# Longer runs of the two feed-forward products in two row groups, a fourth chunk of attention turned by DMA, and one copy of neighbour rows left whole

## The chip, the cores and the metric

The kernel runs on one core of one Trainium2 chip. The metric is device time in microseconds, the median of several executions of the whole program. One further execution was recorded by the hardware profiler; all rows shown below come from that one, and its times count from the start of its span.

## The reference

```python
x = A_x                                            # [1, 2048, 640], float32
xn = layernorm(x)
q, k, v = split(xn @ wqkv)                         # 32 heads of 20
logits = sum_d q[s] * k[s - 2*w] * 20**-0.5        # w = 0..7: a window of 8 rows, every second row
logits = where(s - 2*w >= 0, logits, -1e9)
o = sum_w softmax(logits)[w] * v[s - 2*w]
s = o @ wo                                         # [2048, 640]
h = silu(xn @ w1)                                  # [2048, 1536]
g = silu(h @ w2)                                   # [2048, 640]
return x + s * g
```

Weights are `wqkv` [640, 1920], `wo` [640, 640], `w1` [640, 1536], `w2` [1536, 640].

## The kernel before

**Rows.** The 2048 rows are worked in four groups of 512, `g` = 0 to 3 (two halves of the sequence, times the even and the odd rows, since the window takes every second row). A group lies on 128 partitions with `T` = 4 rows of one parity on each. A row's window reaches seven rows of its parity back, so the last rows of partition p are needed on partitions p+1 and p+2.

**Precision.** Every operand of a product is split into a high and a low float32r part; a product is three matmuls (high·high, low·high, high·low). `TH`/`TL` hold the turned (transposed) input of a group, `OH`/`OL` the turned attention output, `SH`/`SL` the hidden values in a ring of `NS` = 3, `WR` the weights, high and low beside each other, in a ring of `RING` = 7 tiles `w_75` to `w_81`.

**A group.** First the Q/K/V product in four quarters `q` of eight heads each (`qkv_phase`): 20 units of three matmuls, in PSUM banks `acc`; ScalarE then copies a quarter's keys and values to `KV[q]` (L733) and its queries to `Q[q]` (L736, L739). `halo` then copies the last rows of each partition's keys and values to the next two partitions, on SyncE's queue (L751): 4 rows by one partition, 3 rows by two. Each of these two copies is cut in two at row 112 of its rows, so a quarter has four transfers of 112, 15, 112 and 14 partitions. Attention itself (`scores`, `values`) is VectorE's work, in the background, and runs on into the next group. Then the feed-forward (`ffn_phase`): `up` units (L1130 to L1132: w1, into a bank `rot`, of which there are two; ScalarE takes silu twice, L1143 and L1144, VectorE the low part, L1145) and `down` units (L1003, L1005: w2, accumulated over all 12 units in six `acc` banks). Behind the first `up` stands the wo product of the group before (`wo_phase`), and its result is multiplied into the gate tile `G`; GpSimd adds the residual (L1049) from `xr` tiles that SyncE's queue loads (L1048).

**Turning.** A chunk of 128 columns of x or of the attention output `O` is turned in one of two ways. On TensorE (`split_t`, L636): four transposes into a `rot` bank. By DMA (`send`, `join`): ScalarE sorts the chunk into 16-bit halves in one buffer (L668), two DMA transposes on SyncE's queue write a second buffer (L672), ScalarE sorts them back into the first (L681) and rounds the high part (L685), VectorE takes the low part (L686). `ON_DMA` says, by group and quarter, which chunks of the group before are sent and joined when.

**Weights.** In the first rounds weights come raw, are split, and the split form is stored to DRAM (`half_...`, L581 on SyncE's queue); later they are loaded split, by GpSimd's queue (L564), into the tile of the ring that comes free. A load waits until TensorE has used the tile's old content and, where that was a first-round unit, until its store has landed. The five wo units of `g` = 2 are such units (tiles `w_77` to `w_81`).

**Order.** TensorE's order is written out: `units`, from `plan(g)`. All other engines' orders come from a planner in the kernel (`Weave`), which simulates the five engines and eight DMA lanes with its own costs and due times, and adds constraints where TensorE would wait. The engines run their orders as built, each strictly in order.

Of the kernel before, what the change touches and what calls it, by code (L numbers as in the profile page):

```python
# [15 lines left out]
P = 128  # L16
S, D, F, H, DH = 2048, 640, 1536, 32, 20
W = 8
DC, FC = D // P, F // P
NQ = 4  # L20
HQ = H // NQ
CQ = HQ * DH
# [7 lines left out]
CA, CB = 384, 256  # L30
RING = 7
NS = 3
SINGLE = 6
RAW_AHEAD = 10
TURNS = 1
FIRST_AT = 44.0, 60.0
# [6 lines left out]
SUB_LATE = 3  # L43
ADD_LATE = 3
X_BY = {1: 2, 3: 0, 4: 1}
PACE0, PACE = -20.0, 12.0
WARM, WARM2 = 20, 3
HOLD = 3.4
# [11 lines left out]
BY_ACT = (0,)  # L60
IN_PARTS = 2
KEYS_FIRST = ((3, 0),)
QAT = 48
MORE = 32
OAT = 16
# [233 lines left out]
def local_attention_silu_ffn(ctx: ExitStack, tc: tile.TileContext, x, wqkv, wo, w1, w2, out):  # L299
# [9 lines left out]
    xg = x.rearrange("b (g p j) d -> (b g) p j d", p=P, j=J)  # L309
    og = out.rearrange("b (g p j) d -> (b g) p j d", p=P, j=J)  # L310
    OL_AT = {10: 2}
    groups = [(h, par) for h in range(2) for par in range(2)]
    NG = len(groups)

# [38 lines left out]
    SF = sb.tile([P, TOK], F32, name="sf")  # L353
    TURN = sb.tile([P, TOK], F32, name="turn")
# [6 lines left out]
    XP = [("xp", k, h) for k in range(DC) for h in range(2)]  # L361
# [27 lines left out]
    def free_for(old, new):  # L389

        add("DVE", 0.0, lambda: None, [], list(old) + list(new), 0)
# [8 lines left out]
    clock = [0.0]  # L400
# [13 lines left out]
    def plan(g):  # L414

        last = g == NG - 1
        todo = [("w1", 0)] + [("wo", 0)] * (g > 0)
        down = 0  # L420
        f = 1
        while f < FC:
            k = f // 2
            pair = f + 1 < FC and not (last and f > SINGLE)
            if g < TURNS and 1 <= k <= DC and k - 1 not in X_DMA:
                todo.append(("x", k - 1))
            if last and f in OL_AT:
                todo.append(("o", OL_AT[f]))
            if last and f == FC - 1:
                todo.append(("rest", (0, 1)))  # L430
            n = 2 if pair else 1
            todo += [("w1", u) for u in range(f, f + n)]
            f += n
            todo += [("w2", u) for u in range(down, down + n)]
            down += n
        return todo + [("w2", u) for u in range(down, FC)]

# [15 lines left out]
    def store_at(u):  # L455

        return 1 + (u[0] == "wo" or u[0] == "q" and u[2] % 2)
# [15 lines left out]
    for u in units:  # L473
        n = seen[u] = seen.get(u, 0) + 1
        at = store_at(u)
# [8 lines left out]
    def start(i):  # L484

        return QAT if i < first_q else 0

# [203 lines left out]
    def turn_x(c, i, at):  # L691
        keys = [("xin", t) for t in range(T)]
        by = (TURN, ("turn",)) if c not in X_BY else (piece(G, X_BY[c]), ("buf", X_BY[c]))
        to = piece(G, c), ("buf", c)
# [3 lines left out]
    def spare(s, q):  # L698

        return KV[q][:, s, HALO:, :].rearrange("p t m -> p (t m)")[:, :TOK], (("own", "val")[s], q, "x")  # L700

    def lend(s, q, back=False):
        k = ("own", "val")[s]
        lent = [[(k, q, t) for t in range(T)], both((k, q, "x"))]
        free_for(*(lent[::-1] if back else lent))
# [6 lines left out]
    def turn_o(g, c, i, out, into, at=0.0):  # L712

        qs = range(c * P // CQ, ((c + 1) * P - 1) // CQ + 1)
        keys = [("o", q, t) for q in qs for t in (0, 2)]
        xp = [(piece(XIN, k), ("xp", k)) for k in range(DC)]
        by, to = ((xp[0], xp[1]), (xp[2], xp[3]), (xp[4], (TURN, ("turn",))), (xp[1], xp[3]), (xp[0], xp[2]))[c]
        if g < NG - 1:
            by, to = ((TURN, ("turn",)), (SF, ("sf",))) if c % 2 == 0 else (xp[3], xp[4])
        if out:  # L720
            send(O, c, keys, "o", by, to, at)
        if into:
            join(to, by[0].rearrange("p (t n) -> p t n", t=T), both(by[1]), [], i, c, OH[i][:, c, :], OL[i][:, c, :], at)


    def q_keys(q, t):
        return [("q", q, t)] + [("q", q, t, k) for k in range(q if q == NQ - 1 else 0)]
# [14 lines left out]
    def halo(g, q):  # L742
        h, par = groups[g]
        kv = KV[q]
        own = kv[:, :, HALO:, :]
        kown = [(k, q, t) for k in ("kv", "own", "val") for t in range(T)]

        def shift(by, dst, src, tag, s=slice(0, 2), also=()):
            cut = 112
            for a, b in ((0, cut), (cut, P - by)):  # L750
                dma(lambda a=a, b=b: nc.sync.dma_start(kv[a + by:b + by, s, dst], own[a:b, s, src]),  # L751
                    kown, [("halo", q, tag, a, *also)], (b - a) * (s.stop - s.start) * CQ * 4 * (dst.stop - dst.start), clock[0],
                    quick=(g, q) in KEYS_FIRST)
        for part in ((slice(0, 1),), (slice(1, 2), ["v"])) if (g, q) in KEYS_FIRST else ((),):
            shift(1, slice(HALO - T, HALO), slice(0, T), 1, *part)
            shift(2, slice(0, HALO - T), slice(2 * T - HALO, T), 2, *part)
        c = carry[par]
        if h == 0:
            dma(lambda: nc.sync.dma_start(c[:, q], own[P - 2:P]), kown, [("carry", par, q)], 10240, clock[0] + 20)
        else:  # L760
            dma(lambda: nc.sync.dma_start(kv[0:1, :, HALO - T:HALO, :], c[1:2, q]), [("carry", par, q)],
                [("halo", q, 3, 0)], 5120, clock[0])
            dma(lambda: nc.sync.dma_start(kv[0:2, :, 0:HALO - T, :], c[:, q, :, 2 * T - HALO:, :]),
                [("carry", par, q)], [("halo", q, 4, 0)], 7680, clock[0])
# [163 lines left out]
    def qkv_phase(g, i, io):  # L928
        if g == TURNS:
            for c in O_FIRST:  # L930
                by, to = (((TURN, ("turn",)), spare(1, 0)), (spare(0, 1), spare(1, 1)))[c]
                join(to, by[0].rearrange("p (t n) -> p t n", t=T), both(by[1]), [], io, c, OH[io][:, c, :], OL[io][:, c, :])
            for v in ((0, 0), (0, 1), (1, 0), (1, 1)):
                lend(*v, True)
        if g == NG - 1:
            free_for([("xin", t) for t in range(T)], XP)
        if g in ON_DMA and g < NG - 1:
            free_for(["sf"], [("sf", 0), ("sf", 1)])
            free_for([("xin", 2), ("xin", 3)], XP[6:])
        for q in range(NQ):  # L940
            if g == 0 and q == 0:
                ps = first_quarter(i)
            else:
                turn_now(g, q, io)
                ps = [bank() for t in range(T)]
                for c in range(DC):
                    wh, wl, kh, kl = w_next("q", q, c)
                    for t in range(T):
                        o, kp = ps[t]

                        n = wh.shape[-1]

                        def unit(c=c, t=t, o=o, wh=wh, wl=wl, n=n):
                            o = o[:, :n]
                            hi, lo = TH[i][:, c, tsl(t)], TL[i][:, c, tsl(t)]
                            nc.tensor.matmul(o, hi, wh, start=c == 0, stop=False)  # L956
                            nc.tensor.matmul(o, lo, wh, start=False, stop=False)  # L957
                            nc.tensor.matmul(o, hi, wl, start=False, stop=c == DC - 1)  # L958
                        pe(3 * mm(n), unit, t_keys(i, [c], [t]) + [kh, kl], [kp])
                    w_done()  # L960
                    if g:
                        for k in (ON_DMA[g][1] if g in ON_DMA else O_AT).get((q, c), ()):
                            o_chunk(g - 1, k, io)
            if g == 0:
                add("POOL", 2.0, lambda q=q: nc.gpsimd.memset(KV[q][0:2, :, 0:HALO, :], 0.0), ["first"] if q else [],
                    [("halo", q, 1, 0), ("halo", q, 2, 0), ("halo", q, 3, 0), ("halo", q, 4, 0)], 1 + 12 * q)
            for t in range(T):
                evac_qkv(g, q, t, *ps[t])
            halo(g, q)
            scores(g, q)  # L970
            if q:
                values(g, q - 1)
        values(g, NQ - 1)
        turn_now(g, NQ, io)
        if g in ON_DMA and g < NG - 1:
            free_for([("sf", 0), ("sf", 1)], ["sf"])
            free_for(XP[6:], [("xin", 2), ("xin", 3)])

    def turn_now(g, q, io):
        for step in ON_DMA[g][0].get(q, ()) if g in ON_DMA else ():  # L980
            k, into, at = step
            turn_o(g, k, io, not into, into, clock[0] + at)

    def t_keys(i, cs, ts=range(T), kinds=("th", "tl")):
        return [(k, i, c, t) for k in kinds for c in cs for t in ts]

    ON_DMA = {1: ({0: ((0, 0, 4.0),), 1: ((0, 1, 8.0),)}, {(2, 4): (2, 3), (3, 4): (4,)}),
              NG - 2: ({0: ((0, 0, 4.0), (1, 0, 4.0)), 1: ((0, 1, 8.0), (1, 1, 8.0), (2, 0, 4.0)), 2: ((2, 1, 8.0),)},
                       {(2, 4): (3,), (3, 4): (4,)}),
              NG - 1: ({0: ((0, 0, 4.0), (1, 0, 4.0)), 1: ((0, 1, 8.0), (1, 1, 8.0)), 2: ((2, 0, 4.0), (3, 0, 4.0)),  # L990
                        3: ((2, 1, 8.0), (3, 1, 8.0))}, {(3, 4): (4,)})}
    O_AT = {(1, 4): (0,), (2, 4): (2, 3), (3, 4): (4,)}
# [267 lines left out]
```

## Time and profile before

| | |
|---|---|
| median of 3 runs | 624.95 us (624.53 to 624.99) |
| the profiled execution's own time | 624.74 us |
| its span, first to last instruction | 623.0 us |
| mean granted TensorE clock | 1.000 |
| busy: TensorE, VectorE, ScalarE, GpSimd | 617.8, 541.4, 267.7, 114.9 us |
| share of the chain that ended last: TensorE | 98% |
| moved by DMA | 166.86 MB, 268 GB/s |

The profiled execution's time is 1.74 us above its span: what lies before the first and after the last instruction. A row of the chain of work that ended last gives start, length and what ran; a row of the timeline gives start, length, engine, line, operation, tiles, and in brackets the idle time of that engine before it and what ended it. A row of the waits gives the sum, the number and the longest of the waits.

### The profile page before, as it was taken

To read this page: it belongs to the slowest core of one execution; us is meant where nothing else is said; L and a number is where in the kernel's file an instruction comes from. 1 tells how busy PE (TensorE), PEld (TensorE's weight loads), DVE (VectorE), ACT (ScalarE), POOL (GpSimd) and SP (SyncE) were. 2 spreads that over 40 slices of the span, in tenths; PEclk is the share of its full clock that TensorE was granted. 3 is DMA by queue.
4 is the path that set the end of the run, shared out by engine and by line. 5 is a ranking of instruction groups with operands and counts; after the bars stand their busy time and mean duration, and the time that the engine had idled before them with its cause. 6 is when DMAs were issued, how large, how long until landed. Compare 5 with 4: busy or idle time off the path is not lost.

```text
span 623.0 us, 9035 instructions
## 1 busy us (share of the span) xinstructions
PE 617.8 (99%) x3403; PEld 558.4 (90%) x3403; DVE 541.4 (87%) x545; ACT 267.7 (43%) x493; POOL 114.9 (18%) x165
## 2 busy tenths in 40 slices
PE   9999999999999999999999999999999999999997
PEld 7888999998889989999888999999988999999997
DVE  7599899999788999899949999989937999898834
ACT  5445555364545224563543604174644353252220
POOL 4800000001110142111221115112222211111100
PEclk9999999999999999999999999999999999999999
DMA  9999999599999989975999999999699999688652
GB/s 296 310 309 318 331 387 375 195 325 267 297 285 317 322 241 319 234 231 139 227 270 258 351 341 304 162 245 355 171 235 270 286 332 269 197 235 246 184 190 86
DMA packets 102873, 166.86 MB, mean 268 GB/s; under 512 B 34365, under 2 KB 64541, under 8 KB 102829
## 3 DMA queue, kind: packets, MB, share of 16 engines
q1 hardware_dynamic: 76333, 86.56, 52.1%
q0 software_dynamic: 25952, 79.31, 45.3%
q8 instruction: 27, 0.44, 0.3%
q10 hardware_dynamic: 544, 0.41, 0.2%
q14 instruction: 17, 0.14, 0.1%
HBM read 107.91 MB, written 34.16 MB: 228 GB/s over the span
## 4 chain that ended last, share of the span: by engine, by line
PE 98%; DMA 0%; DVE 0%; issue 0%
PE acc L1003 22%; PE acc L1005 15%; PE acc L956 10%; PE acc L958 10%; PE acc L957 10%; PE rot L1131 9%; PE rot L1132 9%; PE rot L1130 9%; PE acc L893 2%; PE rot L636 1%; DMA xin<-in_A_x_dram 0%; PE rot L877 0%; PE rot L1116 0%; DVE st L862 0%; PE rot L836 0%; DVE gate L1084 0%
## 5 line engine op out<-in xcount | busy, mean ns | idle before, releaser
L1003 PE MATMUL acc<-w,sh 128*128 128x384 f32 x384 | 113.2, 334 | 0.0
L956 PE MATMUL acc<-w,th 128*128 128x512 f32 (+2 forms) x300 | 113.0, 377 | 0.0
L958 PE MATMUL acc<-w,th 128*128 128x512 f32 (+2 forms) x300 | 112.9, 376 | 0.0
L957 PE MATMUL acc<-w,tl 128*128 128x512 f32 (+2 forms) x300 | 112.8, 376 | 0.0
L776 DVE TENSOR_TENSOR pr<-q,kv 128x2560 f32<-128x2560 f32 x32 | 90.3, 2821 | 22.8 <-DMA kv<-kv 22.6
L1005 PE MATMUL acc<-w,sh 128*128 128x256 f32 x384 | 107.1, 279 | 0.0
L1143 ACT ACTIVATE sh<-rot 128x512 fp32r<-128x512 f32 x48 | 28.8, 599 | 155.4 <-PE rot L1132 155.3
L1130 PE MATMUL rot<-th,w 128*128 128x512 f32 x240 | 94.4, 393 | 0.0
L1132 PE MATMUL rot<-th,w 128*128 128x512 f32 x240 | 93.9, 391 | 0.0
L1131 PE MATMUL rot<-tl,w 128*128 128x512 f32 x240 | 93.8, 391 | 0.0
L810 DVE TENSOR_TENSOR pr<-q,kv 128x2560 f32<-128x2560 f32 x32 | 91.9, 2871 | 0.8
L779 DVE TENSOR_REDUCE l<-pr 128x128 f32<-128x2560 f32 x32 | 89.9, 2810 | 0.2
L564 POOL DMA_DIRECT2D w<-half_q x52 | 37.4, 719 | 234.5 <-DVE pr L815 97.1
L564 POOL DMA_DIRECT2D w<-half_w x72 | 38.9, 541 | 201.7 <-PE acc L1005 86.4
L815 DVE TENSOR_TENSOR pr<-pr 128x1280 f32<-128x1280 f32 x64 | 74.0, 1155 | 1.2
L1005 PEld LDWEIGHTS acc<-w,sh 128*128 128x128 f32 x384 | 72.2, 188 | 1.0
L1003 PEld LDWEIGHTS acc<-w,sh 128*128 128x128 f32 x384 | 72.1, 188 | 1.0
L958 PEld LDWEIGHTS acc<-w,th 128*128 128x128 f32 x300 | 56.3, 188 | 8.8
L956 PEld LDWEIGHTS acc<-w,th 128*128 128x128 f32 x300 | 56.3, 188 | 8.7
L957 PEld LDWEIGHTS acc<-w,tl 128*128 128x128 f32 x300 | 56.3, 188 | 8.7
L733 ACT ACTIVATE kv<-acc 128x320 f32<-128x320 f32 x64 | 28.0, 440 | 75.9 <-PE acc L958 74.5
L1003 PE MATMUL acc<-w,sl 128*128 128x384 f32 x192 | 57.8, 332 | 0.0
(115 smaller groups left out, 1040.3 us busy)
## 6 DMA issues: line engine op xcount, KB each, us to landing
w<-half_w POOLq DMA_DIRECT2D x72, 640.0 KB, 7.3
w<-half_q POOLq DMA_DIRECT2D x39, 512.0 KB, 5.1
half_w<-w SPq DMA_DIRECT2D x24, 640.0 KB
kv<-kv SPq DMA_DIRECT2D x15, 560.0 KB
w<-half_wo POOLq DMA_DIRECT2D x10, 640.0 KB, 6.9
kv<-kv SPq DMA_DIRECT2D x15, 420.0 KB
gate<-in_B_w_dram SPq DMA_DIRECT2D x16, 320.0 KB
w<-half_q POOLq DMA_DIRECT2D x13, 384.0 KB, 7.4
```

The lines of the kernel that those rows point to most:

```text
L564: add("POOL", 1.0, lambda: nc.gpsimd.dma_start(both, src), [("half", u), ("half", u, "more")], [kh, kl], due + 10, nbytes=2 * n * P * 4)
L776: dve(2560, lambda t=t: nc.vector.tensor_tensor(out=PR, in0=win(qq[:, t:t + 2, :], W, 0), in1=win(kv[:, 0, t:t + 2, :], W, CQ), op=OP.mult ...
L779: dve(2560, lambda t=t: nc.vector.tensor_reduce(out=l[:, t:t + 2].rearrange("p t w h -> p (t w h)"), in_=PR.rearrange("p t w (h d) -> p (t ...
L810: dve(2560, lambda t=t, v=v: nc.vector.tensor_tensor(out=PR.rearrange("p t w (h d) -> p t (w h) d", d=DH), in0=e[:, t:t + 2].rearrange("p ...
L956: nc.tensor.matmul(o, hi, wh, start=c == 0, stop=False)
L957: nc.tensor.matmul(o, lo, wh, start=False, stop=False)
L958: nc.tensor.matmul(o, hi, wl, start=False, stop=c == DC - 1)
L1003: nc.tensor.matmul(a[t][0][:, :CA], st, w[:, :CA], start=first, stop=last)
L1005: nc.tensor.matmul(b[t // 2][0][:, h * CB:(h + 1) * CB], st, w[:, CA:], start=first and h == 0, stop=last, skip_group_check=True)
L1130: nc.tensor.matmul(h, wh[:, cs], TH[i][:, c, :], start=c == 0, stop=False)
L1131: nc.tensor.matmul(h, wh[:, cs], TL[i][:, c, :], start=False, stop=False)
L1132: nc.tensor.matmul(h, wl[:, cs], TH[i][:, c, :], start=False, stop=c == DC - 1)
```

## The change

**Feed-forward order.** The rule that built `plan(g)` is replaced by a table `STEPS[g]` of pairs (ups, downs). Groups 0 and 3 keep their order. Groups 1 and 2 had, behind the first up and wo, runs of two ups and two downs:

```
before: up 1 2, down 0 1, up 3 4, down 2 3, up 5 6, down 4 5, up 7 8, down 6 7, up 9 10, down 8 9, up 11, down 10 11
after:  up 1 2, down 0 1 2, up 3 4 5, down 3 4 5, up 6 7 8, down 6 7 8, up 9 10 11, down 9 10 11
```

**Turning.** During the Q/K/V product of `g` = 2, chunk 3 of the attention of the group before goes by DMA too, so `split_t` is called for chunk 4 alone. For `g` < 3, chunks 1, 2 and 3 use as their two buffers the keys' and the values' half of `KV[1]`, `KV[2]`, `KV[3]` (`LENT`), which the group before has used up, where chunk 1 had used part of `XIN`, and chunk 2 `TURN` and `SF`. `lend` puts the order between these uses and the next copies into `KV` in the planner. The x loads for the next group no longer wait for the part of `XIN`.

**Neighbour rows.** For (`g`, `q`) = (2, 3) the copies of `halo` are not cut: two transfers of 127 and 126 partitions in place of four.

```diff
+LENT = None, 1, 2, 3, None
+UNCUT = ((2,3),)
...
+    STEPS = [
...
+        (((0,), ()), ((1, 2), (0, 1, 2)), ((3, 4, 5), (3, 4, 5)), ((6, 7, 8), (6, 7, 8)), ((9, 10, 11), (9, 10, 11))),
...
-        if g < NG - 1:
-            by, to = ((TURN, ("turn",)), (SF, ("sf",))) if c % 2 == 0 else (xp[3], xp[4])
+        lent = LENT[c] if g < NG - 1 else None
+        if lent is not None:
+            by, to = spare(0, lent), spare(1, lent)
+        elif g < NG - 1:
+            by, to = (TURN, ("turn",)), (SF, ("sf",))
+        if out and lent is not None:
+            for k in range(2):
+                lend(k, lent)
...
+        if into and lent is not None:
+            for k in range(2):
+                lend(k, lent, True)
...
-            for a, b in ((0, cut), (cut, P - by)):
+            for a, b in ((0, P - by),) if (g, q) in UNCUT else ((0, cut), (cut, P - by)):
...
-            free_for([("xin", 2), ("xin", 3)], XP[6:])
...
-              NG - 2: ({0: ((0, 0, 4.0), (1, 0, 4.0)), 1: ((0, 1, 8.0), (1, 1, 8.0), (2, 0, 4.0)), 2: ((2, 1, 8.0),)},
-                       {(2, 4): (3,), (3, 4): (4,)}),
+              NG - 2: ({0: ((0, 0, 4.0), (1, 0, 4.0)), 1: ((0, 1, 8.0), (1, 1, 8.0), (2, 0, 0.0), (3, 0, 10.0)), 2: ((2, 1, 4.0),), 3: ((3, 1, 0.0),)},
+                       {(3, 4): (4,)}),
```

What the planner makes of it, at three places. Line numbers of the kernel after stand 4 to 12 higher than those of the same lines before.

SyncE's queue at the end of the Q/K/V product of `g` = 2, before: the copies of the last quarter's neighbour rows (`kv_96` is `KV[3]`), then the stores of wo units 3 and 4 (`half_wo_170`, `half_wo_171`), with x loads for the residual between.

```order
L1048 DMA xr_109<-in_A_x_dram 128x640
L751 DMA kv_96<-kv_96 112x2x640
L751 DMA kv_96<-kv_96 15x2x640
L751 DMA kv_96<-kv_96 112x2x480
L751 DMA kv_96<-kv_96 14x2x480
L581 DMA half_wo_170<-w_80 128x1280
L1048 DMA xr_107<-in_A_x_dram 128x640
L581 DMA half_wo_171<-w_81 128x1280
```

After:

```order
L1057 DMA xr_109<-in_A_x_dram 128x640
L763 DMA kv_96<-kv_96 127x2x640
L763 DMA kv_96<-kv_96 126x2x480
L585 DMA half_wo_170<-w_80 128x1280
L1057 DMA xr_107<-in_A_x_dram 128x640
L585 DMA half_wo_171<-w_81 128x1280
```

The two stores stay behind the neighbour rows; these are two transfers where there were four.

GpSimd's queue a little later, before: loads of w1 units (`half_w_3_140` is up 3, `half_w_4_141` up 4) and w2 units (`half_w_3_143` is down 3, `half_w_2_142` down 2) into the tiles of the ring, and the residual's additions.

```order
L564 DMA w_79<-half_w_3_140 128x1280
L564 DMA w_80<-half_w_4_141 128x1280
L1049 TENSOR_TENSOR xr_109<-xr_109,gate 128x640
L564 DMA w_75<-half_w_3_143 128x1280
L1049 TENSOR_TENSOR xr_107<-xr_107,gate 128x640
L564 DMA w_81<-half_w_2_142 128x1280
```

After:

```order
L568 DMA w_79<-half_w_2_142 128x1280
L1058 TENSOR_TENSOR xr_109<-xr_109,gate 128x640
L568 DMA w_75<-half_w_5_144 128x1280
L1058 TENSOR_TENSOR xr_107<-xr_107,gate 128x640
L568 DMA w_80<-half_w_3_140 128x1280
L568 DMA w_81<-half_w_4_141 128x1280
```

Tile `w_80`, that of wo unit 3, now takes up 3 where it took up 4, and its load stands behind the second addition, whose x load (`xr_107`) stands behind the store of that unit in SyncE's queue.

ScalarE at the end of the second quarter of `g` = 2 (`kv_94` and `q_98` are this quarter's keys with values and queries, `q_100` the last quarter's), before: chunk 0 is joined, then each bank is copied out whole, one after the other.

```order
L681 ACTIVATE turn<-sf 128x2x512
L685 ACTIVATE th_70<-turn 128x512
L733 ACTIVATE kv_94<-acc_113 128x2x160
L736 ACTIVATE q_98<-acc_113 128x160
L739 ACTIVATE q_100<-acc_113 128x32
L733 ACTIVATE kv_94<-acc_114 128x2x160
```

After:

```order
L685 ACTIVATE kv_94<-kv_94 128x2x512
L689 ACTIVATE th_70<-kv_94 128x512
L672 ACTIVATE kv_96<-o 128x1024
L748 ACTIVATE q_98<-acc_113 128x160
L751 ACTIVATE q_100<-acc_113 128x32
L748 ACTIVATE q_98<-acc_114 128x160
L751 ACTIVATE q_100<-acc_114 128x32
L748 ACTIVATE q_98<-acc_115 128x160
L751 ACTIVATE q_100<-acc_115 128x32
L748 ACTIVATE q_98<-acc_116 128x160
L745 ACTIVATE kv_94<-acc_113 128x2x160
L745 ACTIVATE kv_94<-acc_114 128x2x160
```

Chunk 1 is joined in `KV[1]`, chunk 3 is sent, and the keys and values of all four banks are copied out behind the last bank's queries.

More of the change, by code (lines that the diff above doesn't have):

```diff
@@ L32 @@
 NS = 3
-SINGLE = 6
 RAW_AHEAD = 10
@@ L311, in local_attention_silu_ffn @@
     OL_AT = {10: 2}
+    STEPS = [
[4 rows of a table added]
+    ]
     groups = [(h, par) for h in range(2) for par in range(2)]
@@ L418, in plan @@
         last = g == NG - 1
[L419 to L424, printed above, removed]
+        todo = [("wo", 0)] * (g > 0 and len(STEPS[g][0][1]) > 0)
+        k = 0
+        for ups, downs in STEPS[g]:
             if g < TURNS and 1 <= k <= DC and k - 1 not in X_DMA:
                 todo.append(("x", k - 1))
-            if last and f in OL_AT:
-                todo.append(("o", OL_AT[f]))
-            if last and f == FC - 1:
+            if last and ups[0] in OL_AT:
+                todo.append(("o", OL_AT[ups[0]]))
+            if last and ups[0] == FC - 1:
                 todo.append(("rest", (0, 1)))
[L431 to L436, printed above, removed]
+            todo += [("w1", f) for f in ups] + [("w2", f) for f in downs]
+            if not downs:
+                todo += [("wo", 0)] * (g > 0)
+            else:
+                k += 1
+        return todo
     units = []
@@ L749, in shift @@
             cut = 112
-            for a, b in ((0, cut), (cut, P - by)):
+            for a, b in ((0, P - by),) if (g, q) in UNCUT else ((0, cut), (cut, P - by)):
                 dma(lambda a=a, b=b: nc.sync.dma_start(kv[a + by:b + by, s, dst], own[a:b, s, src]),
-                    kown, [("halo", q, tag, a, *also)], (b - a) * (s.stop - s.start) * CQ * 4 * (dst.stop - dst.start), clock[0],
+                    kown, [("halo", q, tag, k, *also) for k in (0, cut) if a <= k < b], (b - a) * (s.stop - s.start) * CQ * 4 * (dst.stop - dst.start), clock[0],
                     quick=(g, q) in KEYS_FIRST)
@@ L976, in qkv_phase @@
             free_for([("sf", 0), ("sf", 1)], ["sf"])
-            free_for(XP[6:], [("xin", 2), ("xin", 3)])
     def turn_now(g, q, io):
-        for step in ON_DMA[g][0].get(q, ()) if g in ON_DMA else ():
-            k, into, at = step
+        for k, into, at in ON_DMA[g][0].get(q, ()) if g in ON_DMA else ():
             turn_o(g, k, io, not into, into, clock[0] + at)
```

3 rows, old and new, of the table STEPS are left out of this document.

## The prediction

> **What bounds the kernel now.** I read the page's head first, then the chain that ended last, then TensorE's waits.
>
> ```profile
> span 623.0 us, 9035 instructions
> PE 617.8 (99%) x3403; PEld 558.4 (90%) x3403; DVE 541.4 (87%) x545; ACT 267.7 (43%) x493; POOL 114.9 (18%) x165
> ...
> PE 98%; DMA 0%; DVE 0%; issue 0%
> ```
>
> ```profile
> PE rot L849 <- POOL ident masks.py:199: 1.4, 1, 1.4
> ```
>
> The last row is the whole answer to what TensorE waited for: once, 1.4 us, at the start. From then on it is a wall of matmuls. So nothing that other engines save can shorten the time; it changes by what TensorE no longer does, and by any wait that the change puts into the wall. Everything else must be on time, and the question is how much slack each thing has.
>
> **The transposes that go.** One call of L636 leaves TensorE. In the chain it is:
>
> ```profile
> 337.97 0.44 PE rot L636 x4
> ```
>
> Off the path: 0.44 us, all of it, since the chain counts up to the next matmul's slot.
>
> **Longer runs.** Each change from down to up costs TensorE a little. In the chain, a run of two ups (30 matmuls) begins at 369.94, the run of two downs behind it at 376.79, the next up at 383.68:
>
> ```profile
> 369.94 0.23 PE rot L1130
> ...
> 372.03 0.23 PE rot L1130
> ...
> 375.43 0.23 PE rot L1130
> ...
> 376.79 0.18 PE acc L1003
> ...
> 383.68 0.23 PE rot L1130
> ...
> 387.13 0.23 PE rot L1130
> ```
>
> From 372.03 to 375.43 are 15 matmuls: 0.2267 us each, so 30 would be 6.80 us; the run took 6.85. A change thus costs 0.05 us. Groups 1 and 2 have six runs of ups behind wo now and four afterwards: 4 x 0.05 = 0.2 us less in all. Gain of both: 0.64 us.
>
> What could take it back: in a run of three the third up uses the bank of the first, so it starts only when ScalarE has read that bank twice. These reads now end about 1.1 us behind the up:
>
> ```profile
> 387.17 0.60 ACT L1143 ACTIVATE sh<-rot 128x512 fp32r<-128x512 f32 x1 [0.56 <-PE rot L1132]
> 387.66 0.59 ACT L1144 ACTIVATE sf<-rot 128x512 f32<-128x512 f32 x1
> ```
>
> The cover is one up, 3.45 us (383.68 to 387.13), so 2.3 us are left: no cost. A down's inputs are made at least two units earlier, as before.
>
> **The lent buffers.** The second quarter's keys and values (`KV[1]`) can be copied out only when VectorE has taken chunk 1's low part from there. That step stands behind the same addition as chunk 0's does now, at 315.6; the copies come at 322.4:
>
> ```profile
> 315.63 0.68 DVE L686 TENSOR_TENSOR tl<-turn,th 128x512 fp32r<-128x512 f32 x1
> 324.65 2.83 DVE L776 TENSOR_TENSOR pr<-q,kv 128x2560 f32<-128x2560 f32 x1 [8.34 <-DMA kv<-kv]
> ```
>
> ```profile
> 322.37 0.44 ACT L733 ACTIVATE kv<-acc 128x320 f32<-128x320 f32 x1 [8.92 <-PE acc L958]
> ...
> 324.41 0.44 ACT L733 ACTIVATE kv<-acc 128x320 f32<-128x320 f32 x1
> 324.74 0.30 ACT L736 ACTIVATE q<-acc 128x160 f32<-128x160 f32 x1
> ```
>
> VectorE is idle there for 8.34 us, so nothing is lost. But ScalarE now copies the first bank's keys and values behind the fourth bank's queries: not at 322.4 but at about 324.41 + 0.33 (a copy of queries here follows its neighbour by 0.33) = 324.74, done at 325.2. TensorE has finished the fourth bank when ScalarE takes it now, 324.4, and goes on at once; it needs the first bank again as the next quarter's third, six matmuls of 0.227 us later, at 325.8 at the latest and 325.6 at the earliest. Some 0.4 us are left. I cost it at nothing, with a rival below. The joins of chunks 2 and 3 are due 4 and 0 us into their quarters, whose copies begin some 10 us into them; what hides them is that time. The two more DMA transposes load the DMA engines, which TensorE bears now elsewhere: between 387 and 400 they were busy beyond full and moved little, and TensorE did not wait.
>
> ```profile
> 387.00:400.00 13.00, 13.00 (x76) 11.93 (x75) 12.90 (x10) 2.29 (x4) 2.12 (x4) 1.00 1.33 125
> ```
>
> **The neighbour rows in one piece.** This part the forecast hangs on. The copy itself has time: issued at 351, its rows are first used by VectorE at 412. What stands behind it has not. SyncE's queue, VectorE's first scores of that quarter, GpSimd's queue, and the DMA of that stretch (349 to 374):
>
> ```profile
> 350.89 4.24 SPq L751 DMA_DIRECT2D kv<-kv  x4
> 359.86 0.33 SPq L581 DMA_DIRECT2D half_wo<-w  x1
> ```
>
> ```profile
> 412.19 2.82 DVE L776 TENSOR_TENSOR pr<-q,kv 128x2560 f32<-128x2560 f32 x1
> ```
>
> ```profile
> 363.36 0.53 POOL L564 DMA_DIRECT2D w<-half_w  x1 [2.91 <-DVE l L779]
> 373.25 0.53 POOL L564 DMA_DIRECT2D w<-half_w  x1 [9.36 <-DMA kv<-carry]
> 373.80 1.59 POOL L1049 TENSOR_TENSOR xr<-xr,gate 128x640 f32<-128x640 f32 x1
> ```
>
> ```profile
> GB/s 291 410 442 381 477 377 401 418 385 418 406 406 393 430 389 398 320 307 209 254 224 254 310 315 299 303 247 355 356 383 407 402 403 406 422 393 432 414 348 336
> DMA packets 2607, 9.08 MB, mean 363 GB/s; under 512 B 286, under 2 KB 542, under 8 KB 2604
> ...
> w<-half_w POOLq DMA_DIRECT2D x6, 640.0 KB, 8.9
> ...
> kv<-kv SPq DMA_DIRECT2D x1, 560.0 KB
> ...
> kv<-kv SPq DMA_DIRECT2D x1, 75.0 KB
> ```
>
> The load at 373.25 is that into the tile of wo unit 3: it waited 9.36 us for that unit's store, issued at 359.86 behind the neighbour rows. The store thus took 13 us to land, though the DMA engines were never idle: it stood in a queue. So what lengthens the copy ahead of it delays the store, and the load.
>
> Uncut, the copy of 4 rows is one transfer of 127 partitions, 635 KB (560 + 75) as before. How the rows are shared among the 16 engines decides. For that I count completions in the whole run:
>
> ```profile
> DMA packets 102873, 166.86 MB, mean 268 GB/s; under 512 B 34365, under 2 KB 64541, under 8 KB 102829
> ...
> w<-half_w POOLq DMA_DIRECT2D x72, 640.0 KB, 7.3
> w<-half_q POOLq DMA_DIRECT2D x39, 512.0 KB, 5.1
> ...
> kv<-kv SPq DMA_DIRECT2D x15, 75.0 KB
> ...
> kv<-kv SPq DMA_DIRECT2D x15, 52.5 KB
> ...
> half_q<-w SPq DMA_DIRECT2D x9, 32.0 KB
> ...
> gate<-gate SPq DMA_TRANSPOSE x12
> ...
> carry<-kv SPq DMA_DIRECT2D x8, 10.0 KB
> ...
> xr<-in_A_wqkv_dram SPq DMA_DIRECT2D x6, 16.0 KB
> ```
>
> Of the 34365 packets under 512 B, 23552 belong to the 46 transposes (128 partitions of 1 KB, in packets of 256 B: 512 each; the first of their seven rows is shown), and 3328 are rows of 128 or 256 B of small weight pieces (9 x 256, 6 x 128, and 2 x 128 in a row not shown); 7485 remain, the completions. With 16 for each of the 400 plain transfers and, as I take it, 32 for each transpose there would be 7872, 387 more. Those 387 are missing where the rows are few: 17 transfers of 15 rows (the 15 shown and two like them) with 15 completions each, 17 of 14 rows with 14, and 24 to or from the carry with 2 make 17 + 34 + 336 = 387, to the packet. So a transfer runs on as many engines as share its rows equally. All others have 112, 128 or 256 rows, which 16 share equally. 127 is a prime: no number of engines but one shares it equally. The trace has no such transfer, so the two ends are 16 engines (unequal shares, no cost) and one; I take one, because equal shares fit every row of the count.
>
> The Trainium skill's page DMA: Bandwidth & Descriptors, in the section Why a DMA increments its semaphore by 16 and not by 1, says it outright: the number of engines on SyncE's queue is the largest up to 16 that divides the slowest dimension, and 127 partitions go to one. By that rule the sum is the one that follows; the count above agrees with it, and no run here shows 127 rows.
>
> One engine at the stretch's rate of 363 / 16 = 22.7 GB/s needs 650 kB / 22.7 = 28.7 us, where 16 needed 1.8: 26.9 us later. Ends: at the fastest slice of the stretch (477) 20 us, at the run's mean (268) 37 us.
>
> The chain from there: store landed 373.25 + 26.9 = 400.2. GpSimd's load into that tile now stands behind an addition (1.59) whose x load stands behind that store: 401.7. A load lands 7.3 us later (5.1 to 8.9): 409.0. It brings up 3, which TensorE reaches at 369.94 - 0.44 + 6.85 + 1.5 x 6.89 = 386.7. Wait: 22.3 us; low 13, high 34. Behind it the other loads wait too (GpSimd works in order), but they come in a row then, one per 3.45 us of TensorE's need, and everything later is late by the same.
>
> Sum: 624.95 (median; the profiled execution's 624.74, span 623.0 plus 1.74, is 0.21 below it and gives the same differences) - 0.44 - 0.2 + 22.3 = 646.6. I say 646.
>
> **Rivals.**
> 1. *The copy is shared by 16 engines in unequal parts, or lands in time otherwise.* Then nothing waits: 624.3, 0.1% faster, which a measurement of this kernel can hardly tell from no change (0.2%, 1.25 us, is about what it can). For it: no transfer of 127 rows is in the trace. It decides where up 3's load, 7.3 us before 386.7, can still be issued by 379.4: if the copy takes less than 6 us more than now. Chance 0.27. Faster by over 0.2% would need twice the gain that I find; 0.03 of these.
> 2. *One engine, and a wait of 13 to 34 us at up 3*: the forecast, 637 to 658. Against it: a lone queue on an engine may run faster than its share of the stretch. Chance 0.65.
> 3. *A late bank.* The copies of `KV[1]` come more than 0.4 us later than worked out, because chunk 1's turn or the addition ahead of its low part slips, and the third bank of the next quarter holds TensorE; or a run of three waits for a silu that is queued behind a sorting step on ScalarE. Each us late is a us: with 2 to 8 us, 626 to 632. VectorE's idle 8.34 us and the 2.3 us speak against it. Chance 0.08, of which 0.02 stays within 0.2%.
>
> **How the numbers follow.** The likeliest is case 2: 646, its own range 637 to 658. Case 1 ends on the other side, so the whole range runs from 624 to 654: it leaves out the upper part of case 2, about 0.1, and little of case 1. Faster by over 0.2%: 0.03. Same: 0.24 of case 1 and 0.02 of case 3. Slower: 0.65 + 0.06 = 0.71.
>
> **What the profile afterwards would show.** TensorE's waits have, if I am right, a row of L1139 (up) of some 20 us near 387, ended by a weight load, and GpSimd a row of that length or more on the addition or the load; the copy in two issues near 351, and the DMA share low in the slices behind it, since 15 engines idle. If GpSimd's wait stays near 9 us and TensorE has no row near 387, case 1 holds and the step on equal shares is wrong. A wait near 325 or 394 is case 3. One L636 less, and runs of 45 matmuls with one slow start each, show the 0.64 us.

## The result and the profile after

The changed kernel takes 646.07 us (median of 6 runs, 642.08 to 649.17) where the kernel before takes 624.90 on the same chip (6 runs, 624.53 to 625.14): a ratio of 1.033, 95% interval 1.031 to 1.035. Forecast was 646. The profiled execution of the changed kernel took 645.59 us, its span 643.8, 20.8 more than the span before. One execution of experiment 1's kernel (1039.52 us) and one of the kernel cut at 79 rows (1260.94 us) ran their matmuls at about half rate throughout and are left out of the ratios and ranges below. The changed kernel's page begins so, and the chain's shares by engine stand below:

```profile
span 643.8 us, 9024 instructions
PE 619.7 (96%) x3399; PEld 559.7 (87%) x3399; DVE 538.7 (84%) x545; ACT 270.1 (42%) x495; POOL 114.4 (18%) x165
...
PE 93%; DMA 3%; DVE 2%; POOL 0%; ACT 0%; issue 0%; POOLq 0%; SPq 0%
```

TensorE's four matmuls fewer are the transposes of the chunk that DMA turns now. The wall has a hole, and TensorE's waits say where (line, what ended the wait, sum, number, longest):

```profile
PE rot L1139 <- DMA w<-half_w: 18.7, 1, 18.7
PE rot L861 <- POOL ident masks.py:199: 1.4, 1, 1.4
PE rot L889 <- DVE xin L879: 0.5, 1, 0.5
```

The first row is new: L1139 is an up, and it waited for a load of weights. Back from there, GpSimd's queue (the addition L1058, the loads L568), then SyncE's (the copies L763, the stores of wo's parts L585), and the two copies' issues apart from each other (shortest, median, longest in ns):

```profile
373.11 0.57 POOL L568 DMA_DIRECT2D w<-half_w  x1 [0.80 <-PE rot L1141]
398.09 1.52 POOL L1058 TENSOR_TENSOR xr<-xr,gate 128x640 f32<-128x640 f32 x1 [24.41 <-DMA xr<-in_A_x_dram]
399.57 2.16 POOL L568 DMA_DIRECT2D w<-half_w  x4
```

```profile
351.81 31.77 SPq L763 DMA_DIRECT2D kv<-kv  x2
383.76 2.07 SPq L585 DMA_DIRECT2D half_wo<-w  x1
```

```profile
L763 SPq DMA_DIRECT2D kv<-kv x2: 723/15856/30990, 351.8 to 352.6; - x2
```

The load that waited for the store at 373.25 before the change is now issued at 399.57, and up 3 starts when it lands, at 405.2. SyncE's row is the surprise: the two issues took 31.77 us instead of 4.24 for four. The 127-row copy itself is issued in 0.72 us at 351.8; the one behind it, of 126 rows, begins at 352.6 and takes 30.99. So the store goes out at 383.76, 23.9 us later than before (359.86). What GpSimd waited for up to 398.09 was the x load issued behind that store, at 385.88.

The count of completions tells on how many engines the copies ran:

```profile
DMA packets 103915, 167.12 MB, mean 260 GB/s; under 512 B 35407, under 2 KB 65583, under 8 KB 103871
```

Packets under 512 B are 1042 more than the 34365 before. Two transposes more are 2 x (512 + 32) = 1088, and experiment 1, with the copies cut, has these 1088 more. Where four copies gave 16 + 15 + 16 + 14 = 61 completions, two now give n1 + n2 with 1088 - 61 + n1 + n2 = 1042, so n1 + n2 = 15. The trace also records each engine's completion of a transfer by itself: one for the copy of 127 rows, at 394.23, and fourteen for that of 126. So one engine moved 127 rows, and it took until 394.23.

Last, the granted clock. The slices of the page, and three stretches (us, busy and number for PE, PEld, DVE, ACT, POOL; clock; DMA share; GB/s):

```profile
PEclk9999999999999999999999996799999999999999
```

```profile
386.00:405.00 19.00, 0.53 (x4) 0.27 (x2) 1.12 (x2) 1.06 (x1) 6.22 (x8) 0.62 0.60 196
405.00:411.00 6.00, 5.77 (x14) 4.51 (x15) 0.00 (x0) 0.00 (x0) 0.00 (x0) 0.50 1.08 374
411.00:417.00 6.00, 6.00 (x28) 4.95 (x27) 4.20 (x4) 5.16 (x7) 1.06 (x2) 0.99 1.19 320
```

Behind the wait 14 matmuls of 512 columns start in 6 us, in the next 6 us 26 (the row's 28 include two that began before it). The clock is 0.50, then 0.99. By the starts of the matmuls in the trace the wait is 18.9 us and the half-rate ones behind it cost 2.8 more; less the 0.6 that the change saves they make 21.1, where the span grew by 20.8.

### The profile page after: what moved, and what is told of

Its sections match the earlier page's. It is cut to its first block, busy times and chain, and to the rows that moved or that the text cites. A ratio compares the mean times of both kernels' runs of the same rounds, so it can differ in the third digit from the quotient of the medians.

```text
span 643.8 us, 9024 instructions
## 1 busy us (share of the span) xinstructions
PE 619.7 (96%) x3399; PEld 559.7 (87%) x3399; DVE 538.7 (84%) x545; ACT 270.1 (42%) x495; POOL 114.4 (18%) x165
## 4 chain that ended last, share of the span: by engine, by line
PE 93%; DMA 3%; DVE 2%; POOL 0%; ACT 0%; issue 0%; POOLq 0%; SPq 0%
PE acc L1012 21%; PE acc L1014 14%; PE acc L968 10%; PE acc L967 10%; PE acc L969 10%; PE rot L1139 9%; PE rot L1140 8%; PE rot L1141 8%; PE acc L905 2%; DMA xr<-in_A_x_dram 2%; DMA w<-half_w 1%; DVE pr L822 1%; PE rot L640 1%; DVE pr L827 1%; DMA xin<-in_A_x_dram 0%; PE rot L889 0%
## 5 line engine op out<-in xcount | busy, mean ns | idle before, releaser
L1139 PE MATMUL rot<-th,w 128*128 128x512 f32 x240 | 95.8, 399 | 18.7 <-DMA w<-half_w 18.7
L1141 PE MATMUL rot<-th,w 128*128 128x512 f32 x240 | 94.8, 395 | 0.0
L1152 ACT ACTIVATE sh<-rot 128x512 fp32r<-128x512 f32 x48 | 28.7, 598 | 151.4 <-PE rot L1141 151.3
L568 POOL DMA_DIRECT2D w<-half_q x52 | 37.3, 717 | 234.6 <-DVE pr L827 97.2
L568 POOL DMA_DIRECT2D w<-half_w x72 | 38.5, 536 | 203.7 <-PE acc L1014 86.7
L1139 PEld LDWEIGHTS rot<-th,w 128*128 128x128 f32 x240 | 45.7, 191 | 28.0 <-DMA w<-half_w 19.0
L1154 DVE TENSOR_TENSOR sl<-sf,sh 128x512 fp32r<-128x512 f32 x48 | 37.2, 774 | 37.9 <-ACT sf L1153 37.8
```

Of the source, the lines that this page charges most:

```text
L1139: nc.tensor.matmul(h, wh[:, cs], TH[i][:, c, :], start=c == 0, stop=False)
L1141: nc.tensor.matmul(h, wl[:, cs], TH[i][:, c, :], start=False, stop=c == DC - 1)
```

## The experiments

Each ran against the kernel before on its chip, 624.8 to 625.3 us in all of them.

**1. The copy cut again, all else as changed.**

```diff
-UNCUT = ((2,3),)
+UNCUT = ()
```

> The changed kernel with the copy of group 2's quarter 3 cut at row 112 again (112 and 15 rows, 112 and 14), all else as changed: the FFN by threes, chunk 3 turned by DMA, spent keys and values lent. Theory (the whole loss is the uncut copy): TensorE has no wait at up 3 near 387 us, SyncE's four copy issues near 351 us take some 4 us as before, and the time is 624.3 us, 0.64 us under before. Rival (part of the loss comes from the new order or from the lent buffers): a wait of several us is left at the threes or at group 2's first output, and the time stays above 627 us.

Measured: 624.53 us (median), before 625.02; ratio 1.000, interval 0.9988 to 1.0013. The four issues took 4.68 us and the store went out at 360.59:

```profile
353.42 4.68 SPq L763 DMA_DIRECT2D kv<-kv  x4
360.59 0.33 SPq L585 DMA_DIRECT2D half_wo<-w  x1
```

There is no wait near 387. One is left at 443:

```profile
PE acc L1012 <- DMA w<-half_w: 1.7, 1, 1.7
```

The profiled execution took 626.47 us, above the median, so the rest of the change may leave TensorE less slack than before. But the whole loss of 21 us is the uncut copy; the rest of the change cannot be told from nothing in the ratio.

**2. One row cut off: 126 + 1.** The second copy stays uncut.

```diff
-            cut = 112
+            cut = 126 if (g, q) == (2, 3) and by == 1 else 112
```

> The changed kernel with the 127-row copy cut as 126 rows and 1 row; the 126-row copy stays uncut as in the change. Theory (rows are dealt in equal shares to a number of engines that divides them; 127 is prime and goes to one, 126 goes to 14): the issue takes about 1 us instead of 31, TensorE has no wait near 387 us, and the time is 624.3 us. Rival (any copy over 112 rows, or one whose target starts at row 1, is slow): the issue still takes 20 us or more and the time stays above 638 us.

Measured: 624.77 us; ratio 1.0018, interval 0.9991 to 1.0044. Both copies of 126 rows were issued in 1.78 us, and TensorE's only wait is that at the start:

```profile
350.23 1.78 SPq L763 DMA_DIRECT2D kv<-kv  x2
358.44 0.33 SPq L585 DMA_DIRECT2D half_wo<-w  x1
```

Each of the two copies of 126 rows has fourteen completions in the trace. So it is neither "uncut" nor "over 112 rows". One row is worth 21 us, because 127 has no divisor up to 16 but one. The ratio lies above 1 though the median is below that of before, since the ratio is one of means: three of the ten executions took 626.1 to 632.1 us.

**3. The uncut copy alone, in the kernel before.**

```diff
-            for a, b in ((0, cut), (cut, P - by)):
+            for a, b in ((0, P - by),) if (g, q) in UNCUT else ((0, cut), (cut, P - by)):
```

> The kernel before with nothing changed but the uncut copy of group 2's quarter 3 (127 rows, 126 rows). Theory (the copy alone, late store of wo's part 3): SyncE's queue is held some 31 us from 351 us, the store that follows is issued near 384 us instead of 360, the load by GpSimd behind it near 400 us. In the order before, that slot of the ring takes up 4, which TensorE reaches near 387 us as well: a wait of 15 to 20 us there, and 640 to 648 us. Rival (the copy hurts only with the threes, which take the ups earlier): no wait above 3 us, below 629 us.

Measured: 641.56 us; ratio 1.027, interval 1.025 to 1.029.

```profile
350.31 28.17 SPq L752 DMA_DIRECT2D kv<-kv  x2
378.67 2.52 SPq L582 DMA_DIRECT2D half_wo<-w  x1
```

```profile
PE rot L1131 <- DMA w<-half_w: 10.4, 1, 10.4
PE acc L1004 <- DMA w<-half_w: 1.9, 1, 1.9
PE acc L1004 <- DVE sl L1146: 1.6, 1, 1.6
```

The copy does it without the threes or the lent buffers. Its wait was 10.4 us, below the 15 to 20 expected. The queue was held 27.38 us here (the longer of the two issues) and not 31, and the copy landed at 389.58 instead of 394.23. Besides, the load that waits stands ahead of the addition in GpSimd's order of before, not behind it. The time came out as expected because two shorter waits and 2 us of half-rate matmuls were added.

**4. The FFN by threes alone.** Table `STEPS` put into the kernel before.

> The kernel before with the new order of FFN steps alone (groups 1 and 2 by threes); no chunk more by DMA, no buffers lent, copies cut as before. Theory of the sum: four runs of ups fewer, 0.05 us each, 624.7 us. Rival (the threes make TensorE wait for weights or for the gate in some place): 626 us or more, with a wait of 1 us or more in the chain.

Measured: 624.81 us; ratio 1.0021, interval 0.9995 to 1.0047. No wait but that at the start. From the first matmul's start to the last's the trace has 617.41 us, before 617.62: 0.21 less, where four runs at 0.05 had been expected. It shows in one trace; as a time it is below what the runs can tell. The rival is not quite dead either: of the 12 executions four took 626.1 to 633.5 us, where none of the 19 of the kernel before took over 625.6. No trace shows what these four waited for.

**5. The turn and the lent buffers alone.** The cut kernel with runs of two in groups 1 and 2.

> The changed kernel with the old order of FFN steps and the copies cut as before: what is left is chunk 3 of group 2 turned by DMA, and the spent keys and values lent for the turns. Theory of the sum: one group of four transposes on TensorE less, 0.44 us, 624.5 us. Rival (the two DMA turns more, or the buffers that come free later, cost as much elsewhere): 625.0 us or more.

Measured: 628.90 us; ratio 1.008, interval 1.005 to 1.011. My sum failed here, in the way of the prediction's third rival. ScalarE's queue in this kernel, and in the changed one:

```profile
325.48 0.19 ACT L751 ACTIVATE q<-acc 128x32 f32<-128x32 f32 x1
325.55 1.36 ACT L685 ACTIVATE kv<-kv 128x1024 uint16<-128x1024 uint16 x1
326.94 0.63 ACT L689 ACTIVATE th<-kv 128x512 fp32r<-128x512 f32 x1
327.48 1.40 ACT L745 ACTIVATE kv<-acc 128x320 f32<-128x320 f32 x4
```

```profile
324.48 1.42 ACT L745 ACTIVATE kv<-acc 128x320 f32<-128x320 f32 x4
```

```profile
PE acc L967 <- ACT kv L745: 1.4, 1, 1.4
PE acc L967 <- ACT gate L1228: 1.1, 1, 1.1
```

With runs of two the planner put a chunk's join (1.36 + 0.63 us) ahead of the four copies of keys and values, so the banks came free 3 us later (1 us of it because this kernel was already that much behind) and TensorE waited 1.4 us; it waited 1.1 once more at the next group. These are 2.5 of the 4.1 us that the span grew; the rest I have not traced. With the longer runs the planner found an order in which this chunk's turn is free (experiment 1), and that is worth more than what they save themselves. Whether another order would make it free with runs of two was not tried.

**6. The uncut copies behind the stores.** The two issues get an earliest time in the planner and stand behind the stores of wo's parts 3 and 4 and their loads of x:

```diff
-                    quick=(g, q) in KEYS_FIRST)
+                    quick=(g, q) in KEYS_FIRST, at=(clock[0] + 18) * ((g, q) in UNCUT))
```

> The changed kernel with its uncut copies (127 and 126 rows) kept, but issued behind the two stores of wo's parts 3 and 4 and the two loads of x that stood behind them, and ahead of the three stores of out; little else moves on SyncE's queue. Theory (the loss is the late store alone, which reaches TensorE by GpSimd's addition and load): the stores go out near 360 us as before, the queue is held from some 363 to 394 us with only the stores of out and turns behind it, no wait of TensorE near 387 us, 624 to 626 us. Rival (the one busy engine itself slows what TensorE needs, since every load of weights has a share on it): with the 31 us now beside the loads of ups 3 to 11, TensorE waits for weights by 3 us or more in all, and the time is 630 to 640 us.

Measured: 648.11 us; ratio 1.037, interval 1.035 to 1.038: no better. Both theories were wrong in what comes next.

```profile
361.34 44.26 SPq L763 DMA_DIRECT2D kv<-kv  x2
405.73 8.29 SPq L1060 DMA_DIRECT2D out_dram<-xr  x2
414.11 13.35 SPq L676 DMA_TRANSPOSE gate<-turn  x2
```

```profile
ACT xin L685 <- DMA gate<-turn: 30.6, 1, 30.6
...
PE rot L1139 <- ACT sf L1153: 21.3, 1, 21.3
```

The stores went out at 358.88 and 360.18, GpSimd's loads went on to 414 without the long gap, and the wait near 387 is gone, as the theory said. But the queue was held 43.48 us instead of 31, and the turns of the next x went out at 414.11 instead of 403.75. GpSimd's loads had a share on the same engine all along: of a load issued between 372 and 388, 15 of 16 shares land within 6 us and the last 2.7 to 4.1 us behind them. The copy landed only at 423.68, 62 us after its issue, and the first turn, behind it, at 428. ScalarE stood at a join that needs them for 30.6 us, and behind it in its queue the two reads of TensorE's up banks: a wait of 21.3 us, from 414 to 435.6. At these two places of the copy it was another transfer that came late, and the wait was no shorter.

**7. Other primes.** The first copy cut at 113, at 97 and at 79 rows, the rest (14, 30, 48) a number that 14, 15 or 16 engines share; the second copy cut at 112.

```diff
-            cut = 112
+            cut = 113 if (g, q) == (2, 3) and by == 1 else 112
```

> The changed kernel with the first copy of group 2's quarter 3 cut as 113 and 14 rows instead of 127, the second as before the change (112 and 14). 113 is prime. Theory (a prime number of rows goes to one engine): the 113-row issue holds SyncE's queue 31 x 113/127 = 27.6 us, 226 descriptors at one engine's rate; the store follows 3 us earlier than with 127 rows, the wait of TensorE near 387 us is 14 to 16 us, and with the slow matmuls behind it the time is 640 to 643 us. Rival (it is the missing cut, that is the 127 rows with a short rest, and rows are shared unequally: 113 as 15 engines with 7 and one with 8): no wait, 624.3 us.

> As the kernel with 113 and 14 rows, but cut at 97 (prime): 97 and 30 rows for the first copy, 112 and 14 for the second. Theory (one engine takes all 194 pieces, and SyncE's queue is held at the next transfer until that engine has room): the first issue takes under 1 us and the next transfer that needs the engine is held 20 to 23 us (25.47 for 226 pieces, less 32 x 0.11); the store goes out near 376, up 3's load lands near 394 us, TensorE waits 6 to 9 us, and the time is 632 to 638 us. On the clock: matmuls ran at half rate behind waits of 10.5 to 18.9 us and not behind waits of 2 us. If any wait over some us does it, half-rate matmuls (427 ns) follow here too; if it takes about 10 us, none. Rival on the queue (held for a fixed time, not by the number of pieces): held 25 us or more, a wait of 10 us again.

> As the kernels cut at 113 and at 97, now at 79 (prime): 79 and 48 rows for the first copy, 112 and 14 for the second; 158 pieces on one engine. Waits of TensorE so far: 18.7 us with 254 pieces, 10.6 with 226, 14.6 with 194 (loads of GpSimd beside them took part of the engine, so the hold does not follow the pieces alone: 30.99, 25.47 and 25.86 us). Theory: a hold of 14 to 20 us, the store near 370 us, a wait of 2 to 8 us, 627 to 634 us. On the clock: half-rate matmuls (427 ns) followed waits of 10.4 to 21.3 us and not waits of 2 us; a wait of 4 to 8 us tells which side of the bound it is on. Rival (held for some 25 us whatever the number): a wait of 10 us or more.

> The kernel cut at 79 and 48 rows once more, for its profile (its timed runs were 636.0, 638.7 and 642.5 us, where 627 to 634 had been expected). Theory (the hold ends when all but some fixed number of the 158 pieces are through, and GpSimd's loads halve the engine's rate while they run): the 48-row issue is held 15 us or more, the store goes out at 370 us or later and takes 12 us or more to land; a wait of TensorE near 387 us of 3 us or more. Rival (the 158 pieces cost little here, and the 11 to 17 us come from another place, as the wait at the next group's QKV of the kernel with three primes): no wait near 387 us and one of 5 us or more behind 450 us.

Measured: 640.41 us at 113 (636.01 to 646.40; ratio 1.020, 1.018 to 1.023), 640.42 at 97 (1.023, 1.020 to 1.026), 635.99 to 642.50 at 79 (1.023, 1.018 to 1.028) and 633.47 and 634.67 in two further executions (1.013, 1.006 to 1.019), of which the profile at 79 is. Why the first three at 79 took longer is open. At 113, 97 and 79 in turn, the copies' issues on SyncE's queue and TensorE's wait:

```profile
351.32 27.91 SPq L763 DMA_DIRECT2D kv<-kv  x3
```

```profile
PE rot L1139 <- DMA w<-half_w: 10.6, 1, 10.6
```

```profile
353.27 29.06 SPq L763 DMA_DIRECT2D kv<-kv  x4
```

```profile
PE rot L1139 <- DMA w<-half_w: 14.6, 1, 14.6
```

```profile
350.66 20.61 SPq L763 DMA_DIRECT2D kv<-kv  x4
```

```profile
PE rot L1139 <- DMA w<-half_w: 7.2, 1, 7.2
```

The rival at 113 (unequal shares, no wait) falls. In each the first issue took 0.7 us and the one behind it was held (a row of the copy is two pieces of 2560 B):

| rows | pieces on the one engine | next issue held, us | copy landed after, us |
|---|---|---|---|
| 127 (the change) | 254 | 30.99 | 42.4 |
| 127 (experiment 3) | 254 | 27.38 | 39.3 |
| 127 (experiment 6) | 254 | 43.48 | 62.3 |
| 113 | 226 | 25.47 | 37.4 |
| 97 | 194 | 25.86 | 38.2 |
| 79 | 158 | 17.40 | 31.6 |

Each of these copies has one completion. In the trace one such packet takes 0.102 us. The hold ended 11 to 18 us before the copy landed, so it is not the time of the pieces: in the changed kernel some 100 of the 254 were still to come. Neither column follows the pieces alone; what else that engine has to do counts too. The rival of a fixed 25 us falls with the 17.40. My sizes were off: a wait of 14 to 16 us expected at 113 was 10.6, one of 6 to 9 at 97 was 14.6. Two differences between them are on record: at 97 the copy was issued 2 us later (353.3 against 351.3) and landed 2.8 us later, and GpSimd's load stood behind an addition there (issued at 397.12), at 113 ahead of it (392.09).

**8. Three primes.** 61, 53 and 13 rows as three copies.

```diff
-            for a, b in ((0, P - by),) if (g, q) in UNCUT else ((0, cut), (cut, P - by)):
+            for a, b in ((0, 61), (61, 114), (114, 127)) if (g, q) in UNCUT and by == 1 else ((0, cut), (cut, P - by)):
```

> The changed kernel with the 127-row copy issued as three copies of 61, 53 and 13 rows, all prime, and the second copy cut at 112 again. Theory A (a transfer that cannot be shared always goes to the same engine): the same 254 pieces wait on it, SyncE's queue is held 25 to 31 us at the second and third issue, TensorE waits 10 to 19 us, 638 to 647 us. Theory B (such transfers go to engines in turn): three engines with 122, 106 and 26 pieces work beside each other, the hold at the transfer behind them is 12 us or less, the wait at most 3 us, 624 to 628 us.

Measured: 646.44 us; ratio 1.032, interval 1.025 to 1.038. Theory A: the five issues took 29.81 us, 9.9 and 16.9 of it in the second and third. The copy of 61 rows landed at 375.05 and that of 53 rows at 389.14, one after the other and not beside each other: transfers that cannot be shared wait for the same engine. I had the 13 rows wrong: thirteen engines share them (that copy has thirteen completions), so 230 pieces lay on the one engine and not 254.

```profile
350.54 29.81 SPq L763 DMA_DIRECT2D kv<-kv  x5
```

```profile
PE rot L1139 <- DMA w<-half_w: 10.4, 1, 10.4
PE acc L967 <- ACT gate L1228: 6.6, 1, 6.6
```

The second wait, at 468 and again with half-rate matmuls behind it, makes up for the shorter first one.

**9. A candidate: threes in the first group too, copies cut.**

> Candidate: the changed kernel with the copies cut as before and the FFN of the first group by threes as well (chunks of x are then turned behind the threes there). Theory of the sum: one run of ups less than in the cut kernel, 624.4 us, not told from the kernel before by this measurement. Rival (the first group's turns of x, five of them between seven steps before and four now, come late for the next group's QKV): 626 us or more with a wait of TensorE in the first 180 us.

Measured: 637.97 us; ratio 1.020, interval 1.018 to 1.023. Its rival holds, though most waits lie later than I put them:

```profile
PE rot L848 <- DVE o L830: 3.3, 1, 3.3
PE acc L967 <- DMA w<-half_q: 2.4, 1, 2.4
```

The second of these is at 160.8, the first at 602.7, in the last group. Each has half-rate matmuls behind it. How the order of the first group reaches the last was not traced; with this table and this planner, at least, longer runs there are not free. No version beat the kernel before by more than can be measured.

## Why the prediction was right, and where its working was not

- **Gain of 0.64 us: right in size.** Experiment 4 shows 0.21 of the 0.2 for the runs. The kernel of experiment 2, which has all of the change but the prime, has 0.84 us less from first matmul to last. Neither can be told in the times.
- **Equal shares, one engine for 127 rows: right.** The completions (one for 127 rows, fourteen for 126), 126 + 1 against 127, and 113, 97 and 79 show it. The Trainium skill's rule in its page DMA: Bandwidth & Descriptors (section Why a DMA increments its semaphore by 16 and not by 1) is borne out for 127 and 126 rows.
- **"It stood in a queue": right.** I had not foreseen that SyncE's own queue would stand still, held by the next copy's issue, so that the store was issued 23.9 us later. But the trace shows the queue on the engine too. Of the store's 16 shares 15 had landed by 389.52, the last at 397.17; of the x load behind it 15 by 390.89, the last at 397.92, just before GpSimd went on at 398.09. On the one engine the copy's pieces ran from about 363 to 393.7, and that engine's shares of the second copy, the store and the x load followed back to back. An earlier issue would have put the store behind the same pieces; no run shows that alone. The release came at 398.09 instead of 373.25, where I had 400.2. The one engine took some 31 us for the 254 pieces, where I had 28.7.
- **The wait of 22.3 us: mis-sized by 3.4.** Release 2.1 us earlier than worked out; the load landed in 5.6 us (399.57 to 405.2) instead of 7.3, with the DMA engines nearly idle when it was issued; against that TensorE came to up 3 0.35 us earlier than 386.7.
- **What was missing: the clock.** No term held the 2.8 us of half-rate matmuls behind the wait. It nearly made up for the wait that was too long. So 646 came out by luck, with two errors of about 3 us that cancel, and the working is good to about 4 us, not to 0.1.
- **Rival 1** (in time otherwise) fell with the row of L1139. **Rival 3** (a late bank near 325) did not come: the copies ran at 324.48, no row of TensorE there. Experiment 5 shows that it was near: the same buffers with runs of two brought it, 1.4 us at 328.

## What to carry to other kernels

Before merging two DMAs into one, look at the number of rows of the whole: count completions in the trace for the shapes you have, and cut so that the large part has a divisor of 16 or just below. A transfer on one engine costs little where it is issued. It makes late what stands behind it in its queue, first at the next issue and then on the engine itself, so look at everything there; moving it behind the two stores did not mend it here. When a wait is put into a wall of matmuls, add the half-rate ones behind it to the bill.

## What the hardware showed unexpectedly

- **SyncE's queue is held at the issue behind, not at the long transfer.** It took 0.72 us for the copy of 127 rows and 30.99 for the next one. The hold ended when some 100 of the 254 pieces were still to come; which limit that is was not measured.
- **One late share makes a transfer late.** Of each of the five transfers that SyncE's queue issued from 383.76 to 389.19 in the changed kernel, 15 of 16 shares landed within 6 us of the issue and the sixteenth 6.5 to 7.7 us after these.
- **TensorE ran at half rate behind the waits of 2.4 us and more.** Granted clock 0.50 for 6 us behind 18.9 us of waiting, and 0.50 behind the 21.3 us of experiment 6. Behind the 7.2 us of the kernel cut at 79, and the 2.4 us of experiment 9:

```profile
394.00:400.00 6.00, 6.00 (x15) 4.72 (x16) 0.00 (x0) 0.00 (x0) 0.00 (x0) 0.53 1.09 384
```

```profile
160.00:165.00 5.00, 4.22 (x13) 3.34 (x14) 4.03 (x4) 2.81 (x5) 0.00 (x0) 0.72 1.12 280
```

The matmuls behind these waits ran at half rate for 3.3 to 6.1 us, whatever the wait's length from 2.4 to 21 us; none followed the waits below 2 us of experiments 1 and 3. Behind the 2.4 us it did not begin at once: matmuls went on at 160.8, and the half clock lasted from 162.2 to 165.6. In the clock record of the traces the stretches at half clock are 3.41, 10.24, 13.65, 20.48 and 23.89 us long, all multiples of 3.41 (apart from the one behind each program's last matmul). The Trainium skill's page TensorE: Matmul & The Clock Gate, section Part 1: The HAM clock gate (the "warmup" mystery), gives half rate after an idle window of about 3.4 us and full rate after a busy one, the windows running freely. The multiples and the spread of 3.3 to 6.1 us fit such windows; the wait of 2.4 us is shorter than the one that the page asks for, and here the measurement decides.
